# Adding the attention mask of 22 units by a TensorE product, with one maximum over four blocks and exponentials that read PSUM

## The chip, the cores and the metric

The kernel runs on one core of one Trainium2 chip. The metric is the device time of one execution in microseconds (us); lower is better. Each figure for a kernel is the median of some runs, and one more execution of it is profiled.

## What is computed

Three stages follow one another on 2304 tokens (4 sequences of 576) with 8 heads of 64:

```python
scores = scale * q @ k.T                      # scale = 1/8
scores = where(mask, scores, -1e9)            # heads 0-3: the last 32 keys
                                              # heads 4-7: every 4th of the last 128
attn = exp(scores - max(scores)); attn /= sum(attn) + 1e-9
x = attn @ v                                  # 2304 x 512
h = x @ w_in;  x = (h - tanh(h)) @ w_out      # 512 -> 2048 -> 512
h = x @ w_in2; s = h * softmax(h)             # 512 -> 1024
out = ((s - mean(s)) / sqrt(var(s) + 1e-6) * g_ln) @ w_out2
```

## The kernel before

**Units.** The attention is cut into 48 units. A unit holds four blocks; a block is 96 queries against the 128 keys that its mask can reach, so a unit's scores are a tile of 96 partitions x 512 columns (4 blocks x 128 keys), which is one PSUM bank. Eight units make the attention input of one group of 384 tokens, and there are six groups. `load_unit` (lines 123 to 130) brings a unit's transposed q and k (`qkr`, two buffers) and its v by two transfers on the SP queue; because `qkr` has two buffers, the transfer for unit u+2 waits until TensorE has read unit u.

**One unit, step by step** for the first 22 units (`qk_f32`, lines 151 to 166). TensorE multiplies the four blocks as float32 (line 158; the trace counts each as two matmul records, eight to a unit). VectorE then does, block by block, a `tensor_tensor_reduce` (line 163) that reads the scores from PSUM and the mask from SBUF, adds them, scales by -1/8, writes the result to the SBUF tile `p` and its minimum to `nm`; in the trace each is a CUSTOM_DVE_ANT_0 with a READ_ACCUMULATOR2. ScalarE takes the exponential of each block of `p` in place with `nm` as bias and the row sum as accumulator (`sm_exp`, line 198). `sm_norm` (lines 201 to 206) makes the reciprocal of the sum on VectorE and multiplies `p` on GpSimd (POOL, line 205). `tr_pe` transposes the four blocks on TensorE (line 212), ScalarE copies them to SBUF as `pt` (line 218), and `pv_pe` multiplies two units with v (line 233); ScalarE and VectorE write the result in a high and a low part as `x` (lines 241 and 242). The units from 22 on go through `qk_half` with float32r products and keep their own mask step (line 187).

**The constants.** The identity and three masks are one 256 KB transfer into the tile `cst_sb` (line 248), third on the SP queue after unit 0's two transfers.

**Order of the work.** The schedule is manual: each engine executes its instructions in the order in which the program writes them. The first loop (lines 253 to 273, called the first loop below) does units 0 to 7 and, beside them, splits weights: `w_step` (lines 81 to 111) unpacks one 128x512 piece of `w_in` or `w_out` by five or six instructions on VectorE and two on ScalarE. Its PSUM tiles have two banks for scores, two for transposes and two for the v products.

The second loop (line 395 on) is a list of slots. An even slot does `mm1` (line 297, twelve 128x384 products of the first layer for one of 16 column pieces), an odd slot does `mm2` (line 324, twelve products of the second layer, five pieces later). The hidden piece passes through four steps: `tanh` on ScalarE (line 305), `sub` on VectorE (line 308), `hi` on ScalarE (line 311), `lo` on VectorE (line 314). `plan` (line 336 on) puts the attention work of units 8 to 47 into slots: scores in slot p, exponentials in p+1, the transposes of the unit before one or two slots later, the v product one slot after that. All three take their PSUM bank from one pool of two, `a_ps`, in turn. Until about slot 40 each slot also carries `w_step`s. The last stage (lines 424 on) is the second layer pair, again TensorE products with VectorE and ScalarE steps between them.

Of the kernel before, what the change touches and what calls it, by code (L numbers as in the profile page):

```python
# [7 lines left out]
F32 = mybir.dt.float32  # L8
F32R = mybir.dt.float32r
I32 = mybir.dt.int32  # L10
AF = mybir.ActivationFunctionType
ALU = mybir.AluOpType
# [9 lines left out]
NQ, NK = 96, 128  # L22
NU = 8
QC, KC = 4 * NQ, 4 * NK
# [13 lines left out]
def tile_kernel(ctx: ExitStack, tc: tile.TileContext, qk, vw, cst, w_in, w_out, w_in2, w_out2, g_ln, out):  # L38
    nc = tc.nc
    ctx.enter_context(tc.manual_schedule())  # L40

    const = ctx.enter_context(tc.tile_pool(name="const", bufs=1, side="left"))
# [3 lines left out]
    g_p = ctx.enter_context(tc.tile_pool(name="g", bufs=2, side="right"))  # L46
# [3 lines left out]

    y_dr = dr_p.tile([128, KD, NTOK], F32, name="y_dr")

    cst_sb = const.tile([128, 128 + 3 * NK], F32, name="cst_sb")
    ident = cst_sb[:, 0:128]
    masks = cst_sb[:NQ, 128:].rearrange("p (t k) -> p t k", t=3)

    def mask_of(u, j):

        g, r = divmod(u, NU)
        hp, bp = divmod(r, 2)  # L60
        if hp < 2:
            return 0 if (4 * g + 2 * bp + j) % 6 == 0 else 1
        return (0, 2, 1)[g % 3]
# [59 lines left out]
    def load_unit(u):  # L123
        if u < NU * NG:
            r = at_p.tile([128, QC + KC], F32, tag="qkr", name=f"qkr{u}")
            n = 64 if u < NFU else 128
            nc.sync.dma_start(out=r[:n], in_=qk[u, :n])
            v = at_p.tile([NK, 2, 2, D], F32, tag="v", name=f"v{u}", bufs=6)
            nc.sync.dma_start(out=v.rearrange("p b h d -> p (b h d)"), in_=vw[u])
            un[u] = dict(r=r, v=v)  # L130
# [15 lines left out]
    def new_p(u):  # L146
        d = un[u]
        d["p"] = at_p.tile([NQ, 4, NK], F32, tag="p", name=f"p{u}", bufs=3)
        for t in ("nm", "sm", "rs"):
            d[t] = at_p.tile([NQ, 4], F32, tag=t, name=f"{t}{u}")  # L150

    def qk_f32(u, pool, tag):

        d = un[u]
        new_p(u)
        ps = pool.tile([128, 512], F32, tag=tag, name=f"qkp{u}")[:NQ, 0:KC].rearrange("p (b k) -> p b k", b=4)
        for b in range(4):
            nc.tensor.matmul(ps[:, b], d["r"][:64, b * NQ:(b + 1) * NQ],  # L158
                             d["r"][:64, QC + b * NK:QC + (b + 1) * NK], start=True, stop=True)

        def then():
            for b in range(4):
                nc.vector.tensor_tensor_reduce(  # L163
                    out=d["p"][:, b], in0=ps[:, b], in1=masks[:, mask_of(u, b % 2)], op0=ALU.add, op1=ALU.min,
                    scale=-0.125, scalar=3.0e38, accum_out=d["nm"][:, b:b + 1])
        return then

    def qk_half(u, hf, pool, tag):
# [26 lines left out]
    def sm_exp(u, bs=range(4)):  # L195
        d = un[u]
        for b in bs:
            nc.scalar.activation(out=d["p"][:, b], in_=d["p"][:, b], func=AF.Exp, scale=-1.0,  # L198
                                 bias=d["nm"][:, b:b + 1], accum_out=d["sm"][:, b:b + 1])

    def sm_norm(u):
# [43 lines left out]

    st_ps = tc.alloc_tile_pool(name="st_ps", bufs=2, space=PSUM, side="left")
    load_unit(0)
    nc.sync.dma_start(out=cst_sb, in_=cst)
    load_unit(1)
    w_load()  # L250
    load_unit(2)
# [3 lines left out]
    for r in range(NU + 3):  # L255
        t = qk_f32(r, st_ps, "qk") if r < NU else None
        b1 = pv_pe(r - 4, st_ps, "pv") if r % 2 == 0 and 0 <= r - 4 < NU else None
        b2 = tr_pe(r - 2, st_ps, "tr") if 0 <= r - 2 < NU else None
        if r in SW:
            w_step()  # L260
        if t:
            t()
        if back:
            back()
        back = b1
        if t:
            sm_exp(r)
        if 0 <= r - 1 < NU:
            sm_norm(r - 1)
        if b2:  # L270
            b2()
        if r + 3 < NU + 2:
            load_unit(r + 3)
# [67 lines left out]
    def plan():  # L341


        ready = 0
        for u in range(u0, u1 + 2):
            p = 4 * u - 41 if u >= 2 * NU else (2, 6, 8, 12, 14, 16, 18, 20)[u - u0]
            q = p + 2 if u >= 2 * NU or u < u0 + 4 else p + 1
            if u < u1:
                at(p + 2, lambda u=u: preps.extend(prep_unit(u + 1)))
                for i in (2, 3, 3):  # L350
                    at(p + i, lambda: preps.pop(0)() if preps else None)
                if u < NFU:
                    piece(p, lambda u=u: qk_f32(u, a_ps, "at"))
                    at(p + 1, lambda u=u: sm_exp(u))
                    at(p + 2, lambda u=u: sm_norm(u))
                else:
                    piece(p, lambda u=u: qk_half(u, 0, a_ps, "at"))
                    at(p + 2, lambda u=u: sm_exp(u, (0, 1)))
                    piece(p + 1, lambda u=u: qk_half(u, 1, a_ps, "at"))
                    at(p + 3, lambda u=u: sm_exp(u, (2, 3)))  # L360
                    at(p + 4, lambda u=u: sm_norm(u))
                at(p + 1, lambda u=u: load_unit(u + 2))
            if u0 <= u - 1 < u1:
                piece(q, lambda u=u: tr_pe(u - 1, a_ps, "at"))
            if u % 2 and u0 <= u - 3 < u1:
                piece(q + 1, lambda u=u: pv_pe(u - 3, a_ps, "at"))
# [194 lines left out]
def _layout(q, k, v, moe_w_in, moe_w_out, moe2_w_in, moe2_w_out, moe2_g_ln):  # L561
    import numpy as np

    def blocks(a, n, back):


        a = np.asarray(a)
        pl = a[:, :H // 2].transpose(1, 0, 2, 3).reshape(H // 2, B * S, D)
        di = a[:, H // 2:].reshape(B, H // 2, S // DIL, DIL, D).transpose(1, 3, 0, 2, 4)
        di = di.reshape(H // 2, DIL, B * S // DIL, D)  # L570
        o = np.zeros((NG, NU, 2, 2, n, D), a.dtype)
        for g in range(NG):
            for r in range(NU):
                hp, bp = divmod(r, 2)
                for h in range(2):
                    for b in range(2):
                        j = 2 * bp + b
                        if hp < 2:
                            t0, src = g * G + j * NQ - back, pl[2 * hp + h]
                        else:  # L580
                            t0, src = g * NQ - back, di[2 * (hp - 2) + h, j]
                        z = max(0, -t0)
                        o[g, r, h, b, z:] = src[t0 + z:t0 + n]
        return o.reshape(NG * NU, 2, 2, n, D)

    qb, kb, vb = blocks(q, NQ, 0), blocks(k, NK, WIN), blocks(v, NK, WIN)
    qkt = np.concatenate([qb.transpose(0, 4, 1, 2, 3).reshape(NG * NU, D, QC),
                          kb.transpose(0, 4, 1, 2, 3).reshape(NG * NU, D, KC)], axis=2)
    qkt = np.concatenate([qkt, qkt], axis=1)
    vt = vb.transpose(0, 3, 2, 1, 4).reshape(NG * NU, NK, 4 * D)  # L590

    def bits(w):
        return np.ascontiguousarray(w).view(np.int64)

    cst = np.zeros((128, 128 + 3 * NK), np.float32)
    cst[:, :128] = np.eye(128)
    qq, kk = np.arange(128)[:, None], np.arange(NK)[None]
    rel = qq + WIN - kk
    ok = (rel >= 0) & (rel < WIN)
    cross = (qq < NQ // 2) == (kk < WIN + NQ // 2)  # L600
    for i, m in enumerate((ok & (kk >= WIN), ok, ok & cross)):
        cst[:, 128 + i * NK:128 + (i + 1) * NK] = np.where(m, 0.0, -8.0e9)
    return dict(
        qk=qkt, vw=vt, cst=cst,
        w_in=bits(moe_w_in).reshape(KD, 128, NF, 128).transpose(2, 1, 0, 3).reshape(NF, 128, 512),
        w_out=bits(moe_w_out).reshape(NF, 128, DM),
        w_in2=bits(moe2_w_in).reshape(KD, 128, 2, 512).transpose(0, 2, 1, 3),
        w_out2=bits(moe2_w_out).reshape(NF2, 128, DM),
        g_ln=np.asarray(moe2_g_ln).reshape(NF2, 128).T,
    )  # L610
# [20 lines left out]
```

## Time and profile before

| | |
|---|---|
| median of three runs | 747.28 us (745.67 to 747.45) |
| profiled execution, its own time | 747.18 us |
| its span, first to last instruction | 745.4 us |
| TensorE busy | 717.0 us, 96% |
| VectorE busy | 490.8 us, 66% |
| ScalarE busy | 365.5 us, 49% |
| GpSimd busy | 134.7 us, 18% |
| mean granted TensorE clock | 0.995 |

Shares of busy time are averages over stages. The span has three: up to about 47 us the first loop with the loads, up to about 92 us a stretch of the second loop with dense `w_step`s, and the rest, which is TensorE work nearly without a gap. In a row of the timeline the first number is the start, the second the duration in us; durations of neighbours on one engine overlap a little, so the step from start to start is the cost of one. A note in square brackets gives the idle time before the row and what ended it.

### The profile page before, as it was taken

The page shows a single profiled execution, that of the slowest core. Times are in us where ns is not written, and L with a number is a line of the kernel's source. Part 1 is how long each engine was busy: PE and PEld are TensorE (multiplying, and loading weights), DVE is VectorE, ACT ScalarE, POOL GpSimd, SP SyncE. Part 2 cuts the span into 40 slices and gives each one's busy share as a digit, 9 for nine tenths or more (in the row PEclk, how much of TensorE's full clock was granted, in tenths as well). Part 3 has the DMA queues.
Part 4 walks back from the last instruction along what each step waited for, and adds up shares of the span by engine and source line. Part 5 has one row for each costly group of instructions (what it writes and reads, how often), then busy time and mean ns, then how long its engine had stood idle before and what let it go on. Part 6 is the DMA issues. An engine that isn't in the chain of part 4 may idle for free.

```text
span 745.4 us, 11617 instructions
## 1 busy us (share of the span) xinstructions
PE 717.0 (96%) x4168; PEld 653.4 (88%) x4168; DVE 490.8 (66%) x1273; ACT 365.5 (49%) x991; POOL 134.7 (18%) x187
## 2 busy tenths in 40 slices
PE   4968999999999999999999999999999999999997
PEld 3757899999999999999999999999888888888885
DVE  4889888746777777677777535797465555555452
ACT  4856676543444444354444423453255454535444
POOL 1622243201100111111111000020232312322110
PEclk9998999999999999999999999999999999999999
DMA  8857462122222212232212003733201101110001
GB/s 244 238 206 212 141 200 69 40 90 81 64 63 77 66 63 64 65 106 65 65 64 75 1 1 113 241 113 114 72 14 44 57 28 43 58 42 29 15 29 44
DMA packets 30186, 63.61 MB, mean 85 GB/s; under 512 B 2992, under 2 KB 16816, under 8 KB 30128
## 3 DMA queue, kind: packets, MB, share of 16 engines
q1 hardware_dynamic: 26960, 58.15, 24.8%
q10 hardware_dynamic: 3168, 4.72, 1.8%
q8 instruction: 33, 0.54, 0.3%
q14 instruction: 25, 0.20, 0.1%
HBM read 53.42 MB, written 9.44 MB: 84 GB/s over the span
## 4 chain that ended last, share of the span: by engine, by line
PE 88%; DVE 5%; ACT 3%; DMA 2%; POOL 1%; issue 1%; ACTq 0%; SPq 0%; POOLq 0%; DVEq 0%
PE y L324 26%; PE h L297 24%; PE po L524 14%; PE h L462 14%; PE qkp L158 3%; PE pv L233 2%; PE zt L505 2%; PE tp L212 2%; DMA qkr<-in_qk_dram 2%; PE qkp L178 2%; ACT p L198 1%; POOL p L205 1%; DVE gs L314 1%; DVE wi L85 1%; DVE p L163 1%
## 5 line engine op out<-in xcount | busy, mean ns | idle before, releaser
L297 PE MATMUL h<-x,wi 128*128 128x384 f32 x1152 | 223.5, 344 | 1.9 <-DVE x L242 1.8
L324 PE MATMUL y<-gs,wo 128*128 128x384 f32 x1152 | 217.3, 338 | 0.0
L297 PEld LDWEIGHTS h<-x,wi 128*128 128x128 f32 x1152 | 200.6, 191 | 4.0 <-DVE x L242 2.1
L324 PEld LDWEIGHTS y<-gs,wo 128*128 128x128 f32 x1152 | 198.0, 188 | 2.8
L205 POOL TENSOR_TENSOR p<-p,rs 96x512 f32<-96x512 f32 x48 | 77.8, 1621 | 351.3 <-DVE rs L204 259.0
L462 PE MATMUL h<-w2i,yt 128*128 128x512 f32 x432 | 104.9, 397 | 0.0
L524 PE MATMUL po<-w2o,z 128*128 128x512 f32 x432 | 104.1, 396 | 0.1
L524 PEld LDWEIGHTS po<-w2o,z 128*128 128x128 f32 x432 | 80.7, 188 | 20.4 <-ACT z L513 1.9
L513 ACT ACTIVATE z<-zt,gl_sb 128x128 fp32r<-128x128 f32 x144 | 51.0, 367 | 96.9 <-PE zt L505 48.6
L462 PEld LDWEIGHTS h<-w2i,yt 128*128 128x128 f32 x432 | 79.7, 187 | 18.4
L305 ACT ACTIVATE t<-h 128x384 f32<-128x384 f32 x96 | 47.1, 491 | 96.8 <-PE h L297 90.7
L514 DVE SCALAR_TENSOR_TENSOR z<-zt,gl_sb,z 128x128 fp32r<-128x128 f32 x144 | 48.9, 350 | 69.2 <-ACT z L513 69.2
L198 ACT ACTIVATE p<-p,nm 96x128 f32<-96x128 f32 x192 | 75.0, 392 | 32.8 <-DVE nm L163 32.8
L314 DVE TENSOR_TENSOR gs<-t,gs 128x384 fp32r<-128x384 f32 x96 | 75.7, 788 | 20.9 <-ACT gs L311 18.8
L308 DVE TENSOR_TENSOR t<-h,t 128x384 f32<-128x384 f32 x96 | 52.9, 551 | 32.4 <-ACT t L305 32.4
L311 ACT CAST gs<-t 128x384 fp32r<-128x384 f32 x96 | 49.2, 512 | 47.6 <-DVE t L308 47.5
L158 PE MATMUL qkp<-qkr 64*96 64x128 f32 x176 | 32.5, 340 | 15.6 <-DMA qkr<-in_qk_dram 11.2
L158 PEld LDWEIGHTS qkp<-qkr 64*96 64x96 f32 x176 | 26.7, 206 | 20.7 <-DMA qkr<-in_qk_dram 6.8
L242 DVE TENSOR_TENSOR x<-pv,x 128x384 fp32r<-128x384 f32 x24 | 16.9, 703 | 40.0 <-ACT x L241 40.0
L389 POOL TENSOR_TENSOR yt<-yr,yt 128x1024 fp32r<-128x1024 f32 x9 | 24.3, 2697 | 85.8 <-DVE yt L388 85.8
L479 DVE SCALAR_TENSOR_TENSOR u<-h,e 128x1024 f32<-128x1024 f32 x18 | 22.0, 1225 | 23.9 <-ACT e L478 23.9
L198 ACT ACTIVATION_READ_ACCUMULATOR p<-p,nm 96x1 f32 x192 | 36.2, 188 | 0.0
(68 smaller groups left out, 688.8 us busy)
## 6 DMA issues: line engine op xcount, KB each, us to landing
qkr<-in_qk_dram SPq DMA_DIRECT2D x26, 448.0 KB, 3.3
raw_wi<-in_w_in_dram SPq DMA_DIRECT2D x16, 512.0 KB, 6.4
raw_wo<-in_w_out_dram SPq DMA_DIRECT2D x16, 512.0 KB, 5.4
v<-in_vw_dram SPq DMA_DIRECT2D x48, 128.0 KB, 3.2
qkr<-in_qk_dram SPq DMA_DIRECT2D x22, 224.0 KB, 3.6
y_dr<-ys ACTq DMA_DIRECT2D x6, 768.0 KB, 3.8
yr<-y_dr SPq DMA_DIRECT2D x9, 512.0 KB, 4.4
out_dram<-o SPq DMA_DIRECT2D x18, 256.0 KB, 2.0
```

Source lines behind the costliest of these rows:

```text
L158: nc.tensor.matmul(ps[:, b], d["r"][:64, b * NQ:(b + 1) * NQ], d["r"][:64, QC + b * NK:QC + (b + 1) * NK], start=True, stop=True)
L198: nc.scalar.activation(out=d["p"][:, b], in_=d["p"][:, b], func=AF.Exp, scale=-1.0, bias=d["nm"][:, b:b + 1], accum_out=d["sm"][:, b:b + 1])
L205: nc.gpsimd.tensor_tensor(out=d["p"], in0=d["p"], in1=d["rs"].unsqueeze(2).to_broadcast([NQ, 4, NK]), op=ALU.mult)
L297: nc.tensor.matmul(ps, w[:, a, k * 128:(k + 1) * 128], xt[g, k][:, b], start=(n == 0), stop=(n == 3 * KD - 1))
L308: nc.vector.tensor_tensor(out=t, in0=ps, in1=t, op=ALU.subtract)
L311: nc.scalar.copy(out=gs[:, 0], in_=t)
L314: nc.vector.tensor_tensor(out=gs[:, 1], in0=t, in1=gs[:, 0].bitcast(F32), op=ALU.subtract)
L324: nc.tensor.matmul(yb[g][m], wo[c][:, a, m * 128:(m + 1) * 128], gs[:, b], start=(c == 0 and i == 0), stop=(c == NF - 1 and i == 2))
L462: nc.tensor.matmul(ps[:, n * 512:(n + 1) * 512], y[:, a, k, o:o + TT], w2i[2 * k + n][:, b], start=(q == 0), stop=(q == 3 * KD - 1))
L513: nc.scalar.activation(out=z[:, 0, c], in_=pp[n][:, j], func=AF.Copy, scale=gc)
L514: nc.vector.scalar_tensor_tensor(out=z[:, 1, c], in0=pp[n][:, j], scalar=gc, in1=z[:, 0, c].bitcast(F32), op0=ALU.mult, op1=ALU.subtract)
L524: nc.tensor.matmul(po, z[:, a, j], w2o[j][:, b], start=(q == 0), stop=(q == 3 * NF2 - 1))
```

## The change

Three things are changed, for units 0 to 21 alone. The mask is added by a TensorE product: a 96x96 identity times the masks, 512 columns in float32r, opens the PSUM accumulation, and the four float32 products accumulate onto it. VectorE takes one maximum over the last axis of the whole 96x512 tile (negated, into the four columns of `nm`) and multiplies `nm` by 1/8. The exponentials read the scores from PSUM with scale 1/8, and write `p`. For the product the constants must be of the float32r type, so they now land in a temporary tile `cst_f` and VectorE copies them to `cst_sb`. The mask value is -2^33 in place of -8e9.

```diff
-    cst_sb = const.tile([128, 128 + 3 * NK], F32, name="cst_sb")
-    ident = cst_sb[:, 0:128]
-    masks = cst_sb[:NQ, 128:].rearrange("p (t k) -> p t k", t=3)
+    cst_sb = const.tile([128, 128 + 3 * NK], F32R, name="cst_sb")
+    ident = cst_sb[:, 0:128].bitcast(F32)
+    rmasks = cst_sb[:NQ, 128:].rearrange("p (t k) -> p t k", t=3)
+    masks = cst_sb[:NQ, 128:].bitcast(F32).rearrange("p (t k) -> p t k", t=3)
...
         ps = pool.tile([128, 512], F32, tag=tag, name=f"qkp{u}")[:NQ, 0:KC].rearrange("p (b k) -> p b k", b=4)
+        m0, m1 = mask_of(u, 0), mask_of(u, 1)
+        if m0 != m1:
+            ms = rmasks[:, m0:m0 + 2].unsqueeze(1).to_broadcast([NQ, 2, 2, NK])
+        else:
+            ms = rmasks[:, m0:m0 + 1].to_broadcast([NQ, 4, NK])
+        nc.tensor.matmul(ps, cst_sb[:NQ, 0:NQ], ms, start=True, stop=False)
         for b in range(4):
             nc.tensor.matmul(ps[:, b], d["r"][:64, b * NQ:(b + 1) * NQ],
-                             d["r"][:64, QC + b * NK:QC + (b + 1) * NK], start=True, stop=True)
+                             d["r"][:64, QC + b * NK:QC + (b + 1) * NK], start=False, stop=(b == 3))
+        d["sc"] = ps
 
         def then():
-            for b in range(4):
-                nc.vector.tensor_tensor_reduce(
-                    out=d["p"][:, b], in0=ps[:, b], in1=masks[:, mask_of(u, b % 2)], op0=ALU.add, op1=ALU.min,
-                    scale=-0.125, scalar=3.0e38, accum_out=d["nm"][:, b:b + 1])
+            nc.vector.tensor_reduce(out=d["nm"], in_=ps, axis=mybir.AxisListType.X, op=ALU.max, negate=True)
+            nc.vector.tensor_scalar(out=d["nm"], in0=d["nm"], scalar1=0.125, scalar2=None, op0=ALU.mult)
         return then
...
         for b in bs:
-            nc.scalar.activation(out=d["p"][:, b], in_=d["p"][:, b], func=AF.Exp, scale=-1.0,
+            src, sc = (d["sc"], 0.125) if "sc" in d else (d["p"], -1.0)
+            nc.scalar.activation(out=d["p"][:, b], in_=src[:, b], func=AF.Exp, scale=sc,
                                  bias=d["nm"][:, b:b + 1], accum_out=d["sm"][:, b:b + 1])
...
-    nc.sync.dma_start(out=cst_sb, in_=cst)
+    cst_f = g_p.tile([128, 128 + 3 * NK], F32, tag="ys", name="cst_f", bufs=1)
+    nc.sync.dma_start(out=cst_f, in_=cst)
+    nc.vector.tensor_copy(out=cst_sb, in_=cst_f)
```

How the instructions stand on the engines shows at three places. A name such as `DVE_49` in square brackets is the semaphore of an engine or of a DMA queue on which the instruction waits.

First TensorE at the start of the program, units 0 and 1. Before:

```order
L158 MATMUL qkp_111<-qkr_86 96x128 [waits DMAHW0_49]
L158 MATMUL qkp_111<-qkr_86 96x128 x3
L158 MATMUL qkp_132<-qkr_91 96x128 [waits DMAHW3_49]
L158 MATMUL qkp_132<-qkr_91 96x128 x3
L158 MATMUL qkp_163<-qkr_97 96x128 [waits DMAHW6_49,DVE_49]
```

With the change:

```order
L164 MATMUL qkp_113<-cst_sb 96x512 [waits DVE_49]
L166 MATMUL qkp_113<-qkr_86 96x128 [waits DMAHW0_49]
L166 MATMUL qkp_113<-qkr_86 96x128 x3
L164 MATMUL qkp_133<-cst_sb 96x512
L166 MATMUL qkp_133<-qkr_93 96x128 [waits DMAHW3_49]
L164 MATMUL qkp_163<-cst_sb 96x512 [waits DVE_49,Activation_49]
```

Unit 0's products, which waited for unit 0's transfer alone, now stand behind a product that waits for VectorE's copy of the constants; and unit 2's bank is now waited for from ScalarE as well.

Second ScalarE at the start. Before:

```order
L198 ACT_TABLE_LOAD
L198 ACTIVATE p_107,sm_109<-p_107,nm_108 96x128 [waits DVE_49] x4
L92 ACTIVATE wa_wi_137<-raw_wi_95 128x512 [waits DMAHW5_49]
L198 ACTIVATE p_128,sm_130<-p_128,nm_129 96x128 [waits DVE_49] x4
L92 ACTIVATE wa_wi_174<-raw_wi_101 128x512 [waits DMAHW0_49]
```

With the change:

```order
L206 ACT_TABLE_LOAD [waits DVE_49]
L206 ACTIVATE p_109,sm_111<-qkp_113,nm_110 96x128 [waits PE_49]
L206 ACTIVATE p_109,sm_111<-qkp_113,nm_110 96x128 x3
L94 ACTIVATE wa_wi_139<-raw_wi_97 128x512 [waits DMAHW5_49]
L206 ACTIVATE p_129,sm_131<-qkp_133,nm_130 96x128 [waits DVE_49,PE_49]
```

The load of the function table waited for nothing and now carries the wait for the first maximum; the four exponentials of a unit, which waited each for its own block, now wait once for all four.

Third TensorE in the second loop, where the scores of unit 10 take the bank of unit 9 (`qkp_722` before, `qkp_714` with the change), and the transposes of unit 11 the bank of unit 12's scores (`tp_956` and `tp_947`). Before:

```order
L158 MATMUL qkp_722<-qkr_598 96x128 [waits DMAHW7_49,DVE_49]
L158 MATMUL qkp_722<-qkr_598 96x128 x3
...
L158 MATMUL qkp_913<-qkr_754 96x128 [waits DMAHW7_49,DVE_49]
L158 MATMUL qkp_913<-qkr_754 96x128 x3
...
L212 MATMUL tp_956<-cst_sb,p_840 128x96 [waits DVE_49,Pool_49]
```

With the change:

```order
L164 MATMUL qkp_714<-cst_sb 96x512 [waits DVE_49,Activation_49]
L166 MATMUL qkp_714<-qkr_591 96x128 [waits DMAHW7_49]
L166 MATMUL qkp_714<-qkr_591 96x128 x3
...
L164 MATMUL qkp_903<-cst_sb 96x512 [waits DVE_49,Activation_49]
...
L220 MATMUL tp_947<-cst_sb,p_831 128x96 [waits DVE_49,Activation_49,Pool_49]
```

Where TensorE waited for VectorE to have read a bank, it now also waits for ScalarE's exponentials out of it.

## Rows read from the trace of the kernel before

**Rows 1.** The page, its busy times and the span in 40 slices.
```profile
PE 717.0 (96%) x4168; PEld 653.4 (88%) x4168; DVE 490.8 (66%) x1273; ACT 365.5 (49%) x991; POOL 134.7 (18%) x187
...
PE   4968999999999999999999999999999999999997
```

**Rows 2.** Busy times by stretch: start:end, length, PE, PEld, DVE, ACT, POOL, clock, DMA, GB/s.
```profile
15.00:20.00 5.00, 1.97 (x9) 1.72 (x9) 2.81 (x14) 3.08 (x11) 2.27 (x1) 1.00 1.05 263
...
25.00:30.00 5.00, 4.60 (x22) 3.81 (x21) 4.27 (x18) 4.48 (x17) 3.34 (x2) 1.00 0.82 234
...
75.00:80.00 5.00, 5.00 (x31) 4.61 (x30) 4.92 (x11) 3.59 (x9) 1.04 (x1) 1.00 0.32 129
...
100.00:200.00 100.00, 100.00 (x659) 94.88 (x658) 69.71 (x205) 54.14 (x159) 20.99 (x11) 1.00 0.27 81
```

**Rows 3.** Timeline of TensorE, 0 to 62 us.
```profile
4.38 2.02 PE L158 MATMUL qkp<-qkr 64*96 64x128 f32 x8 [4.38 <-DMA qkr<-in_qk_dram]
...
18.04 1.99 PE L158 MATMUL qkp<-qkr 64*96 64x128 f32 x8 [3.21 <-DMA qkr<-in_qk_dram]
...
47.42 6.69 PE L297 MATMUL h<-x,wi 128*128 128x384 f32 x24 [1.83 <-DVE x L242]
54.05 1.11 PE L158 MATMUL qkp<-qkr 64*96 64x128 f32 x8
```

**Rows 4.** Timeline of the SP queue, unit 2's load.
```profile
6.43 0.47 SPq L127 DMA_DIRECT2D qkr<-in_qk_dram  x1
```

**Rows 5.** Timeline of VectorE: unit 0, then unit 9 in the second loop.
```profile
6.80 0.29 DVE L163 CUSTOM_DVE_ANT_0 p<-qkp,cst_sb 96x128 f32<-96x128 f32 x1 [6.80 <-DMA cst_sb<-in_cst_dram]
...
66.25 0.28 DVE L163 CUSTOM_DVE_ANT_0 p<-qkp,cst_sb 96x128 f32<-96x128 f32 x1
...
67.10 0.55 DVE L308 TENSOR_TENSOR t<-h,t 128x384 f32<-128x384 f32 x1
68.71 0.56 DVE L314 TENSOR_TENSOR gs<-t,gs 128x384 fp32r<-128x384 f32 x1 [1.07 <-ACT gs L311]
```

**Rows 6.** Timeline of ScalarE: start, unit 9, unit 13.
```profile
0.72 1.28 ACT L198 ACT_TABLE_LOAD   x1 [0.72 <-PEq L619]
...
66.63 0.40 ACT L198 ACTIVATE p<-p,nm 96x128 f32<-96x128 f32 x1 [1.86 <-DVE nm L163]
...
68.19 0.49 ACT L311 CAST gs<-t 128x384 fp32r<-128x384 f32 x1
...
94.26 0.39 ACT L198 ACTIVATE p<-p,nm 96x128 f32<-96x128 f32 x1
```

**Rows 7.** Timeline of TensorE, 60 to 130 us.
```profile
67.23 2.02 PE L158 MATMUL qkp<-qkr 64*96 64x128 f32 x8 [3.62 <-DVE nm L163]
...
88.28 0.52 PE L212 MATMUL tp<-cst_sb,p 96*128 96x96 f32 x4 [0.66 <-POOL p L205]
...
91.55 1.11 PE L158 MATMUL qkp<-qkr 64*96 64x128 f32 x8 [0.64 <-ACT pt L218]
...
97.32 0.88 PE L233 MATMUL pv<-pt,v 128*64 128x96 f32 x16
```

**Rows 8.** Groups by line and shape: names, shapes, count, busy us, mean ns.
```profile
L462 PE MATMUL h<-w2i,yt 128*128 128x512 f32 x432 | 104.9, 397 | 0.0
...
L477 DVE TENSOR_REDUCE sml<-h 128x1 f32<-128x1024 f32 x18 | 22.0, 1221 | 9.4 <-PE h L462 9.4
...
L163 DVE CUSTOM_DVE_ANT_0 p<-qkp,cst_sb 96x128 f32<-96x128 f32 x88 | 20.1, 282 | 12.6 <-DMA cst_sb<-in_cst_dram 6.8 <-PE qkp L158 5.8
...
L139 DVE CAST qks<-qkr 128x896 fp32r<-128x896 f32 x26 | 16.0, 614 | 0.0
...
L203 DVE TENSOR_SCALAR rs<-sm 96x4 f32<-96x4 f32 x48 | 8.4, 174 | 0.0
...
L163 DVE DVE_READ_ACCUMULATOR2_ANT nm<- 96x1 f32 x88 | 7.0, 79 | 0.0
...
L330 DVE COPY ys<-y 128x384 f32<-128x384 f32 x12 | 6.6, 556 | 8.5 <-PE y L324 8.5
```

More of the change, by code (lines that the diff above doesn't have):

```diff
@@ L601, in _layout @@
     for i, m in enumerate((ok & (kk >= WIN), ok, ok & cross)):
-        cst[:, 128 + i * NK:128 + (i + 1) * NK] = np.where(m, 0.0, -8.0e9)
+        cst[:, 128 + i * NK:128 + (i + 1) * NK] = np.where(m, 0.0, -2.0 ** 33)
     return dict(
```

## The prediction

> **What bounds the kernel now.** I read the page's shares first: TensorE is 96% busy over the span, and only its first five slices or so fall short [rows 1]. The table by stretch says when: from 100 to 200 us TensorE is busy for 100.00 of 100 us, so whatever is added to it there is paid in full. Before that other things bind: the DMA engines' share is 1.05 at 15 to 20 us, and VectorE is busy 4.92 of 5 us at 75 to 80 [rows 2]. So I price the change in three places.
>
> In the first 47 us the timeline of TensorE shows products that wait for transfers (unit 0's at 4.38 us, unit 3's at 18.04 us after 3.21 idle), and the hidden products begin at 47.42 us [rows 3]. From there to about 92 us VectorE is the bound: its instructions follow one another, and where it idles it is for ScalarE (1.07 us before line 314 at 68.71) [rows 5], while TensorE waits 3.62 us for unit 9's bank and 0.64 us for a copy that ScalarE makes late [rows 7]. After 91.55 us TensorE is the bound.
>
> **VectorE's step itself: nothing.** It falls from eight instructions to two. The old step takes from 66.25 to 67.10, 0.85 us from its start to the next instruction [rows 5]. The new maximum reads 512 columns of PSUM: the copy of 384 takes 556 ns and the reduction of 1024 takes 1221 [rows 8], so 1.04 ns per column and 556 + 128 x 1.04 = 0.69 us; the multiplication of 96x4 is like line 203, 0.17 [rows 8]. Together 0.86, less some 0.04 of overlap with the next: 0.82. That is 0.03 us less per unit.
>
> The Trainium skill, "VectorE: DVE Perf Modes", Rules for kernel authors, says to minimize the number of operations on VectorE. By that rule eight to two is a clear gain. The rows say that the old eight overlap; the rule's result is a rival below.
>
> **The start: 3.2 us.** The first maximum had to wait for the constants until 6.80 us [rows 5], while unit 0's products were long done. Now the products stand behind them too. The cast of 128x512 takes about 0.4 us (614 ns for 896 columns [rows 8]). The mask product is 128x512 in line 462, 104.9 / 432 = 0.243 us [rows 8]. Early TensorE work runs at half speed: the eight records of line 158 take 1.99 and 2.02 us here and 1.11 us at 54.05 [rows 3]. The granted clock in the table reads 1.00 (2.4 GHz) for all of these [rows 2]; I go by the durations, and price a mask product at 0.44 us before 47 us. So unit 0's products run from 6.80 + 0.4 + 0.44 + 0.1 = 7.7 and end at 9.7 us; they ended at 6.40 [rows 3]. Behind that end the SP queue holds unit 2's load, issued at 6.43 [rows 4], and behind it three 512 KB weight loads: all 3.3 us later. Bounds for what reaches unit 3's load are 0 (the DMA engines move what is queued and lose nothing) and 3.3. They are full at 15 to 20 us [rows 2], which is near the upper end, but the 512 KB queued last is 2.0 us of work at that row's 263 GB/s, so they do not stand for all of it: I take 2.1.
>
> From unit 3 on the path runs through TensorE (units 4 and 5), VectorE, POOL, then unit 7 on TensorE again; it meets three more mask products, 3 x 0.44 = 1.3, less 0.2 of waits that they fill: 1.1. Sum 3.2; bounds 1.1 and 4.6. The table load, 1.28 us at 0.72 us [rows 6], now starts after the first maximum. It delays unit 0's exponentials and with them unit 2's bank; I cost it at nothing, since unit 3 waits for its load meanwhile. Without that cover it is up to 1.3 more.
>
> **The VectorE stretch, units 8 to 12: 2.9 us.** The old exponentials begin 0.38 us after the first of the four steps (66.25 to 66.63 [rows 5, 6]), since block 0 needs its own minimum only. Now they need 0.69 + 0.03 + 0.17 + 0.04 = 0.93 us: 0.55 later. Behind the four exponentials ScalarE's queue holds line 311 (68.19 [rows 6]), and VectorE's line 314 waits for that (68.71 after 1.07 idle [rows 5]). I went through the same timelines for all five: units 9 and 11 show the idle of 1.1 us, and for the other three ScalarE's line 311 ends no earlier than VectorE is free. So each costs 0.55 - 0.03 = 0.52, 2.6 in all. Bounds are 0 and 0.55 each.
>
> The held banks come on top. Unit 10's products took unit 9's bank when VectorE had read it, at 67.23 [rows 7]; now they wait for the exponentials, 1.6 us longer. TensorE runs behind nothing there, and the five mask products of this stretch (0.24 each, 0.44 while slow) hide in the same waits, so both cost nothing; if that cover were gone, they are 1.4 for the products. One place reaches the path: the transposes at 88.28 [rows 7] take unit 12's bank, now free some 1.6 us later, and twelve products stand between them and 91.55; of the idle 0.66 and 0.64 there nothing is left and I count 0.3 more. Sum 2.9; bounds 0 and 4.5.
>
> **TensorE from 92 us on: 2.2 us.** Units 13 to 21 are nine mask products at 0.243, on a TensorE without gaps. Bounds 0.21 each (a share by columns of the same row's busy time, were some of it start-up) and 0.30.
>
> **Sum:** 3.2 + 2.9 + 2.2 = 8.3 us. On the profiled execution's own 747.18 us that is 755.5; it is 0.1 us below the median of the runs, so no correction.
>
> **Rivals.**
> 1. *The start is absorbed* by the transfer queue; only the mask products on the path stay, 1.1 in place of 3.2: 753.4 us. For it: 2.0 us of data are still queued when the load is late. Against: TensorE's 3.21 us wait for unit 3's load [rows 3].
> 2. *Held banks stall TensorE after 92 us as well.* Unit 13's last exponential begins at 94.26 [rows 6] and ends at 94.65; the v product that takes its bank next starts at 97.32 [rows 7]. That is 2.7 us of room, of which 0.55 goes. About four places are of this kind. If each lost 1 us, it would be 759.5. It decides once ScalarE lags by over 2 us. The Trainium skill, "PSUM: Partial Sum Buffer", Summary: rules for kernel authors, says to evacuate promptly, which speaks against this change; by rows 6 and 7 the delay fits in that room.
> 3. *TensorE comes up to full speed early.* The mask product is a full-width pass of 512 columns between short ones. If durations from unit 3 on were those of 54.05 us, units 3, 4, 5 and 7 on the path give back 0.9 each (1.99 against 1.11), the first 24 hidden products 2.0 (6.69 us [rows 3] against 4.72 for 24 at full speed, twice line 297's step of 2.36), three mask products 0.6: 6.2, so 749.3. Against: at 25 to 30 us TensorE is busy for 4.60 of 5 us [rows 2] and still slow.
> 4. *Not slower: VectorE's instruction count is what costs.* If the eight old instructions occupied 4 x (0.282 + 0.079) [rows 8] = 1.44 us and the new two 0.86, each unit would save 0.58. Over five units the VectorE stretch would give 2.9 back in place of costing 2.9, and the two maxima on the path of the first loop 1.2: 8.3 - 5.8 - 1.2 = 1.3, so 748.5, no change that can be told. It decides if the timeline's 0.85 understates the step. Against: start-to-start times are what the next instruction sees. That is the result by the skill's rule on the number of operations, named above.
>
> **How the numbers follow.** A measurement of this kernel can tell about 0.3% (2.2 us) from no change. The forecast has 0.60, with a range of its own from 752.5 to 758; rival 1 has 0.14, rival 2 0.10, rival 3 0.07, rival 4 0.06, and 0.03 is left for faster by more, two of them together. Slower is 0.60 + 0.14 + 0.10 = 0.84; rivals 3 and 4 make 0.13 for the same; faster 0.03. The range from 751.5 to 759 holds the forecast, rival 1 and half of rival 2, about 0.79.
>
> **What would show it.** Each step has its mark: the first product on TensorE near 7.3 us and unit 0's end near 9.7; ACT_TABLE_LOAD near 10.7; unit 3's four products near 20; the first hidden product near 50.6; a TENSOR_REDUCE of 0.69 us; exponentials that begin 0.9 us after it starts; unit 13's products near 97.6; 22 mask products, the last nine 0.24 us apart from their neighbours. I am wrong if the hidden products start before 49 us, if VectorE's line 314 does not slip behind the exponentials, or if TensorE shows idle time over 1 us after 100 us.

## The result and the profile after

The change takes 755.1 us (median of four runs, 753.51 to 757.42) beside 746.89 for the kernel before: a ratio of 1.0111 with a 95% interval from 1.0094 to 1.0127, so 8.2 us slower, between 7.0 and 9.5. The forecast was 755.5, slower.

The profiled execution of the change is the slowest of its four runs, 757.42 us with a span of 755.6. Its time lies 2.3 us above their median. That matters below: where those 2.3 us lie has to be found before its rows are read.

First the page of the change: busy times, then the same TensorE slices as in [rows 1].

```profile
PE 724.5 (96%) x4190; PEld 657.0 (87%) x4190; DVE 489.4 (65%) x1142; ACT 361.4 (48%) x991; POOL 134.7 (18%) x187
...
PE   4767999999999999999999999999999999999997
```

TensorE has its 22 products more (4168 to 4190) and is 7.5 us longer busy. VectorE runs 131 instructions fewer, and is busy for 1.4 us less: eight records became two, and almost no time went with them. The new instructions in the groups by line (shapes, count, busy us, mean ns, idle before):

```profile
L206 ACT ACTIVATE p<-qkp,nm 96x128 f32<-96x128 f32 x88 | 30.9, 357 | 41.4 <-DVE nm L172 32.9 <-DVE rs L211 7.5 <-PE tp L220 0.9
...
L171 DVE TENSOR_REDUCE nm<-qkp 96x4 f32<-96x512 f32 x22 | 15.0, 682 | 13.6 <-PE qkp L166 13.5
L164 PE MATMUL qkp<-cst_sb 96*96 96x512 f32 x22 | 11.9, 541 | 12.9 <-DVE cst_sb L258 6.5 <-ACT p L206 6.4
```

The timeline of TensorE in the change, from its first product to unit 14's (the mask product is line 164, the four score products line 166, the hidden layer line 307):

```profile
6.53 0.74 PE L164 MATMUL qkp<-cst_sb 96*96 96x512 f32 x1 [6.53 <-DVE cst_sb L258]
7.20 2.02 PE L166 MATMUL qkp<-qkr 64*96 64x128 f32 x8
...
13.06 0.74 PE L164 MATMUL qkp<-cst_sb 96*96 96x512 f32 x1 [1.23 <-ACT p L206]
...
21.55 2.02 PE L166 MATMUL qkp<-qkr 64*96 64x128 f32 x8 [4.54 <-DMA qkr<-in_qk_dram]
...
25.98 2.02 PE L166 MATMUL qkp<-qkr 64*96 64x128 f32 x8 [1.15 <-DMA qkr<-in_qk_dram]
...
52.90 6.38 PE L307 MATMUL h<-x,wi 128*128 128x384 f32 x24 [1.84 <-DVE x L250]
...
74.71 0.74 PE L164 MATMUL qkp<-cst_sb 96*96 96x512 f32 x1 [5.18 <-ACT p L206]
...
99.77 0.40 PE L164 MATMUL qkp<-cst_sb 96*96 96x512 f32 x1
```

Against [rows 3]: unit 0's products start at 7.20 instead of 4.38, unit 3's (21.55) still wait for their load, and unit 4's (25.98) now wait for theirs too. Before, unit 4's waited for no load:

```profile
21.02 1.99 PE L158 MATMUL qkp<-qkr 64*96 64x128 f32 x8 [0.17 <-DVE nm L163]
```

The hidden products begin at 52.90, not 47.42. On the SP queue (start, duration) unit 2's load, behind the first score products, goes out at 9.24 instead of 6.43 [rows 4], unit 4's at 15.78:

```profile
9.24 0.47 SPq L129 DMA_DIRECT2D qkr<-in_qk_dram  x1
...
15.78 0.47 SPq L129 DMA_DIRECT2D qkr<-in_qk_dram  x1
```

The table by stretch of the change (columns as in [rows 2]) shows what that does. The DMA engines stand idle from 8 to 10 us, at a share of 0.01; from 15 to 20 us they are full again, but over the first 20 us they moved 202 GB/s in the mean, beside 246 before, so the gap isn't made up by then. The last row is the stretch without gaps on TensorE, as before:

```profile
8.00:10.00 2.00, 2.00 (x8) 1.29 (x8) 0.71 (x2) 0.00 (x0) 0.00 (x0) 1.00 0.01 4
15.00:20.00 5.00, 2.01 (x9) 1.23 (x7) 4.15 (x10) 2.38 (x10) 1.39 (x1) 1.00 1.05 278
...
100.00:200.00 100.00, 100.00 (x658) 93.66 (x657) 68.63 (x155) 53.20 (x161) 23.66 (x11) 1.00 0.30 89
```

VectorE around unit 9's maximum in the change, the place of [rows 5]:

```profile
72.17 0.68 DVE L171 TENSOR_REDUCE nm<-qkp 96x4 f32<-96x512 f32 x1
72.88 0.17 DVE L172 TENSOR_SCALAR nm<-nm 96x4 f32<-96x4 f32 x1
72.96 0.55 DVE L318 TENSOR_TENSOR t<-h,t 128x384 f32<-128x384 f32 x1
75.09 0.56 DVE L324 TENSOR_TENSOR gs<-t,gs 128x384 fp32r<-128x384 f32 x1 [1.58 <-ACT gs L321]
...
82.12 0.56 DVE L324 TENSOR_TENSOR gs<-t,gs 128x384 fp32r<-128x384 f32 x1 [0.54 <-ACT gs L321]
...
91.71 0.56 DVE L324 TENSOR_TENSOR gs<-t,gs 128x384 fp32r<-128x384 f32 x1 [1.59 <-ACT gs L321]
```

Before, line 314 of unit 11, which stands in the place of the last of these rows:

```profile
84.33 0.56 DVE L314 TENSOR_TENSOR gs<-t,gs 128x384 fp32r<-128x384 f32 x1 [1.10 <-ACT gs L311]
```

And ScalarE in the change, at the start and at that same maximum [rows 6]:

```profile
10.22 1.28 ACT L206 ACT_TABLE_LOAD   x1 [10.22 <-DVE nm L172]
...
73.17 0.36 ACT L206 ACTIVATE p<-qkp,nm 96x128 f32<-96x128 f32 x1 [2.47 <-DVE nm L172]
...
74.55 0.51 ACT L321 CAST gs<-t 128x384 fp32r<-128x384 f32 x1
```

The new step holds VectorE from 72.17 to 72.96, 0.79 us, where the old one took 0.85. Its exponentials begin 1.00 us after its start (old: 0.38), the cast of line 321 waits behind them, and VectorE's line 324 (314 before) stands idle for 1.58 us instead of 1.07.

Two marks on TensorE divide the span into three: the first hidden product, and unit 13's first product (scores before, mask now). For before they are 47.42 and 91.55 of a span of 745.4; for the change 52.90 and 99.77 of 755.6.

| us | start | to unit 13 | rest | sum |
|---|---|---|---|---|
| before | 47.42 | 44.13 | 653.85 | 745.4 |
| the change | 52.90 | 46.87 | 655.83 | 755.6 |
| difference | 5.5 | 2.7 | 2.0 | 10.2 |
| predicted | 3.2 | 2.9 | 2.2 | 8.3 |

Two terms came out as forecast. The start is 2.3 us too long, just what this execution is above its median, but one profile can't say whether that is the change or chance. The experiments are on that, and on which part of the change pays for each stretch.

### The profile page after: what moved, and what is told of

Read it like the earlier page. It is cut to its first block, busy times and chain, and to the rows that moved or that the text cites. A ratio compares the mean times of both kernels' runs of the same rounds, so it can differ in the third digit from the quotient of the medians.

```text
span 755.6 us, 11526 instructions
## 1 busy us (share of the span) xinstructions
PE 724.5 (96%) x4190; PEld 657.0 (87%) x4190; DVE 489.4 (65%) x1142; ACT 361.4 (48%) x991; POOL 134.7 (18%) x187
## 4 chain that ended last, share of the span: by engine, by line
PE 90%; DVE 3%; ACT 2%; DMA 2%; POOL 1%; issue 1%; ACTq 0%; SPq 0%; POOLq 0%
PE y L334 26%; PE h L307 25%; PE po L534 13%; PE h L472 13%; PE qkp L166 3%; PE pv L241 2%; PE zt L515 2%; PE tp L220 2%; PE qkp L185 2%; DMA qkr<-in_qk_dram 1%; PE qkp L164 1%; ACT p L206 1%; POOL p L213 1%; DMA cst_f<-in_cst_dram 1%; DVE nm L171 0%
## 5 line engine op out<-in xcount | busy, mean ns | idle before, releaser
L206 ACT ACTIVATE p<-qkp,nm 96x128 f32<-96x128 f32 x88 | 30.9, 357 | 41.4 <-DVE nm L172 32.9
L206 ACT ACTIVATE p<-p,nm 96x128 f32<-96x128 f32 x104 | 40.7, 393 | 0.0
```

The source lines that it names most:

```text
L206: nc.scalar.activation(out=d["p"][:, b], in_=src[:, b], func=AF.Exp, scale=sc, bias=d["nm"][:, b:b + 1], accum_out=d["sm"][:, b:b + 1])
```

## The experiments

Changes of the median are against the kernel before in the same session: 747.39 us (23 runs) for the first four experiments, 746.8 (21) for the next four, 747.63 (7) for the last three.

**Parts of the change by unit.** A set NEW holds the units that go the new way; the others keep the four old products and the four fused additions with their minima.

```diff
+        if u not in NEW:
+            for b in range(4):
+                nc.tensor.matmul(ps[:, b], d["r"][:64, b * NQ:(b + 1) * NQ],
+                                 d["r"][:64, QC + b * NK:QC + (b + 1) * NK], start=True, stop=True)
...
+            return old
```

*NEW = range(0, 8): the start alone.*

> The new path for units 0 to 7 only; units 8 to 21 as before. Theory (the terms add up, and the start is the term that was sized too small): this kernel alone carries the start. In the profile of the change the hidden products begin at 52.90 us instead of 47.42, so about +5.5 us against the kernel before, first hidden product near 52.9. Rival (the sum on record): +3.2 us, first hidden product near 50.6. Rival (the start costs nothing by itself, the whole loss is in the second loop): within 1 us of before.

749.75 us, ratio 1.0031 [1.0018, 1.0043], +2.4. The first hidden product starts at 49.40, not at 52.90, and unit 3's products wait 1.92 us for their load:

```profile
19.27 2.02 PE L178 MATMUL qkp<-qkr 64*96 64x128 f32 x8 [1.92 <-DMA qkr<-in_qk_dram]
```

That is the start as forecast or a little less, and not the 5.5 of the profile of the change.

*NEW = range(8, 22): all but the start.*

> The new path for units 8 to 21 only; units 0 to 7 as before, the cast of the constants stays. Theory: the start is as before (first hidden product within 0.7 us of 47.42), the VectorE stretch costs 2.7 to 2.9 and the nine products behind it 2.0 to 2.2, so +4.7 to +5.1 us. Rival (held banks or late exponentials cost nothing, only products count): +2.2. Rival (all of the loss is the start): within 1 us of before.

752.2 us, 1.0064 [1.0048, 1.0079], +4.8, as expected; the stretch to unit 13 is 46.69. The first hidden product stands at 48.25, 0.83 us behind that of the kernel before where I had expected it within 0.7. With the start alone it makes 7.2, inside the interval of the whole change.

*NEW = range(13, 22): the units where TensorE is the bound.*

> The new path for units 13 to 21 only, which all lie behind 92 us, where TensorE has no gaps. Theory: nine mask products of 0.22 to 0.243 us, +2.0 to +2.2 us. Rival (late exponentials and held banks stall TensorE there too): over +4 us and waits of mask products for exponentials in the trace. Rival (the mask products find gaps): within 0.7 us of before.

749.46 us, 1.0029 [1.0018, 1.0039], +2.1: nine mask products at 0.23.

*The same nine units without their mask product,* so that their scores stay unmasked.

```diff
-        nc.tensor.matmul(ps, cst_sb[:NQ, 0:NQ], ms, start=True, stop=False)
...
-                start=False, stop=(b == 3))
+                start=True, stop=True)
```

> As the new path for units 13 to 21 only, but without the mask product there, so that these units' scores are unmasked; one maximum and exponentials out of PSUM stay. Theory: the products were the whole cost behind 92 us, so within 0.7 us of before. Rival (held banks): what is left of the cost of the run with the products stays, +1 us or more.

746.98 us, 0.9996 [0.9984, 1.0008]: nothing left. So after 92 us the product is the whole cost. The late exponentials and the banks that they hold cost nothing there that these runs can tell, and the fewer instructions on VectorE bring nothing there.

**The start.** *NEW = range(1, 22): unit 0 the old way.*

> The change, but unit 0 goes the old way: its products do not wait for the constants, its exponentials do not read PSUM, and the function table is loaded at the start. Theory: the start's 5.5 us fall to the mask products on the path, 3 x 0.44 less filled waits, about 1.1; first hidden product near 48.5 to 49; total +5.5 to +6.5 us against before (the change: +8.2). Rival (the start's cost lies in the mask products and the late exponentials of units 1 to 7): no better than the change by more than 1 us.

752.65 us, 1.0071 [1.0055, 1.0088], +5.85: 2.35 less than the change, as expected. In its SP queue unit 2's load is back where it was, and on its TensorE the hidden products begin at 48.79:

```profile
6.03 0.47 SPq L130 DMA_DIRECT2D qkr<-in_qk_dram  x1
```
```profile
48.79 7.17 PE L319 MATMUL h<-x,wi 128*128 128x384 f32 x24 [1.84 <-DVE x L262]
```

Unit 0 going the new way is thus most of the start's cost. The edit gives back its old products, its load order, its additions and its exponentials together, so that it is the load behind the products that costs is read from the rows, not parted from the rest by a run.

*The table loaded early,* by an exponential of 96x1 ahead of everything:

```diff
+    tb = at_p.tile([NQ, 1], F32, tag="tb", name="tb", bufs=1)
+    nc.vector.memset(tb, 0.0)
+    nc.scalar.activation(out=tb, in_=tb, func=AF.Exp)
     load_unit(0)
```

> The change, with one exponential of a 96x1 tile of zeros ahead of the program's first transfer, so that the function table is loaded at the start instead of behind the first maximum. Theory (in the profile of the change the chain runs through the table load, unit 0's exponentials, unit 2's bank and unit 4's transfer): unit 2's products end 1.2 to 1.3 us earlier, unit 4's arrive earlier by 1 us or more, and the time falls by 1.0 to 1.5 us against the change, to about +7 over before. By the prediction on record (the load is covered by unit 3's wait): no change against the change, +8.2.

754.82 us, 1.0102 [1.0088, 1.0116], +8.0: no gain that can be told, although the interval (6.6 to 8.7) still holds the +7 of my theory. The marks decide against it: the first hidden product starts at 50.67, within the range of the change's own starts (52.90, and 50.12 in its second profile below). The table is loaded at 0.72 us, as before the change, and ScalarE's first exponential starts right behind the maximum; but TensorE's unit 3 still waits for its transfer:

```profile
0.72 1.28 ACT L257 ACT_TABLE_LOAD   x1 [0.72 <-PEq L632]
...
10.52 0.36 ACT L206 ACTIVATE p<-qkp,nm 96x128 f32<-96x128 f32 x1 [8.30 <-DVE nm L172]
```
```profile
20.42 2.02 PE L166 MATMUL qkp<-qkr 64*96 64x128 f32 x8 [4.14 <-DMA qkr<-in_qk_dram]
```

TensorE reaches this wait 1.56 us earlier than in the second profile of the change (unit 3's mask product at 15.55 and 17.11), and waits 4.14 us there instead of 2.16: what the early table gave went into the wait for the data. The cover that the prediction named held.

*Weights out of the way, in the kernel before:* two of the three 512 KB weight loads ahead of the loop move behind the unit loads of its passes 3 and 5.

```diff
-    for _ in range(3):
-        w_load()
+    w_load()
...
         if r + 3 < NU + 2:
             load_unit(r + 3)
+        if r in (3, 5):
+            w_load()
```

> The kernel before, with two of the three weight loads that stand together behind unit 2's transfer moved behind units 6 and 8, so that 1 MB less is queued ahead of unit 3's transfer. Theory (in the first 20 us the transfers bind and a late or crowded transfer of q and k reaches the path in full): unit 3's products start 2 to 4 us earlier than 18.04, the first hidden product 1 to 3 us earlier, 1 to 3 us less in all. Rival (what is moved is only paid later, since VectorE or the loads bind from 20 us on): no change, or slower by up to 3 us because weight pieces come late.

745.41 us (11 runs), 0.9983 [0.9974, 0.9992]: 1.4 us faster than the kernel before, and the fastest kernel here. On its TensorE, unit 3's products come 3.48 us earlier than in [rows 3], and half of that reaches the hidden products:

```profile
14.56 1.99 PE L158 MATMUL qkp<-qkr 64*96 64x128 f32 x8 [0.24 <-DMA qkr<-in_qk_dram]
...
45.74 6.21 PE L298 MATMUL h<-x,wi 128*128 128x384 f32 x24 [1.84 <-DVE x L242]
```

So before the change, unit 3's load does stand on the path, and the weights in the queue are part of it.

*The change again,* and *the same spread in the change* (the diff above on it), in one session:

> The change itself once more, with another profile. Theory (52.90 us for the first hidden product is a draw of the transfers: kernels that share its start gave 50.27 and 49.40, kernels that share the old start 47.42 to 48.34): the first hidden product comes between 49.4 and 51.5, behind unit 4's transfer, and the stretch from there to unit 13 takes 46.9 us as in the first profile, within 0.3. Rival (52.90 is what the change does): again above 52.

> The change, with the same two weight loads moved back as in the run on the kernel before. Theory (what the start costs is a late transfer that is then crowded): unit 3's products start within 17 us instead of 19.3 to 21.6 in the profiles of the change's start so far, the first hidden product near 48.5 to 49.5 instead of 49.4 to 52.9, and the time is 1.5 to 3 us less than the change, +5 to +6.5 over before. Rival (mask products and late exponentials set the start): no change against the change.

The change again: 754.76 us, 1.01 [1.008, 1.0121]. Its stretch to unit 13 is 46.86 and its rest 655.82, both within 0.01 us of the first profile; its start is not. On TensorE:

```profile
20.00 2.02 PE L166 MATMUL qkp<-qkr 64*96 64x128 f32 x8 [2.16 <-DMA qkr<-in_qk_dram]
...
23.20 2.02 PE L166 MATMUL qkp<-qkr 64*96 64x128 f32 x8
...
50.12 6.49 PE L307 MATMUL h<-x,wi 128*128 128x384 f32 x24 [1.83 <-DVE x L250]
```

Unit 4's products no longer wait. The 52.90 of the first profile was one slow draw of the transfers: there unit 4's load took 10.15 us in the chain of waits.

With the spread, 753.61 us, 1.0087 [1.007, 1.0104]: 6.0 above the kernel before, as expected, but only 1.15 below the change of that session, where I had 1.5 to 3, with run times that overlap. The marks were missed too: I had unit 3's products within 17 us and the hidden ones at 48.5 to 49.5, and they start at 18.58 and 50.51. This profile is of the slowest of the four runs, 1.4 us above their median. Its chain of waits (start, us, what) shows what held it up:

```profile
13.92 7.10 DMA raw_wi<-in_w_in_dram
21.05 0.59 DVE wy_wi L95
21.64 0.60 DVE wy_wi L103
22.23 0.60 DVE wy_wi L107
22.84 0.61 DVE nm L171
```

The weight tile, loaded later, now holds up VectorE's weight work, and unit 3's maximum stands behind that. In this execution what the units' loads gave was lost to the weights: the wait moved. Whether the faster three runs lost as much is not shown.

**The stretch of VectorE, units 8 to 12.** *Without the maximum* (no maximum, no multiplication, exponentials with bias 0 in units 8 to 12):

```diff
-            nc.vector.tensor_reduce(out=d["nm"], in_=ps, axis=mybir.AxisListType.X, op=ALU.max, negate=True)
+            if u not in NOMAX:
+                nc.vector.tensor_reduce(out=d["nm"], in_=ps, axis=mybir.AxisListType.X, op=ALU.max, negate=True)
...
-                bias=d["nm"][:, b:b + 1]
+                bias=0.0 if u in NOMAX else d["nm"][:, b:b + 1]
```

> The change, but units 8 to 12 leave out the maximum: VectorE does nothing for them, and their exponentials start when the products end, with bias 0. Theory (in the stretch to 92 us VectorE is the bound, and each unit's exponentials delay ScalarE's line for the high part, on which VectorE waits): five times VectorE's 0.82 us plus up to five times the 0.55 us of lateness come off, so 4 to 7 us less than the change, +1 to +4 over before; VectorE's idle before the low part falls below 0.6 us per unit. Rival (TensorE's waits for held banks bound the stretch): under 2 us less than the change.

748.22 us, 1.0015 [1.0004, 1.0026], +1.4: 6.8 us less than the change, as expected. The stretch shrinks to 40.41 us, by 6.5. Five steps of 0.79 are 4.0 of that. The rest is less idle time of VectorE before the low part: 4.8 us over the five units in the change, 1.2 here, where units 9 and 11 alone still wait, 0.58 each. Together that is 1.1 us more than the stretch lost, so not all of it reached TensorE's mark.

```profile
69.24 0.56 DVE L326 TENSOR_TENSOR gs<-t,gs 128x384 fp32r<-128x384 f32 x1 [0.58 <-ACT gs L323]
```

*With the maximum, but exponentials that don't use it* (only the bias is 0):

```diff
-                bias=d["nm"][:, b:b + 1]
+                bias=0.0 if u in FREE else d["nm"][:, b:b + 1]
```

> The change, but the exponentials of units 8 to 12 use bias 0 and so do not wait for the maximum, which VectorE still takes for them. It parts lateness from VectorE's time, both of which the run without the maximum took away together (6.9 us less than the change). Theory (lateness is on the path in each of the five units): the exponentials no longer hold up ScalarE's line for the high part, so VectorE's idle before the low part goes from 0.54 and 1.59 us to near 0: 2.7 to 5 us less than the change. Rival (VectorE's own time alone counts): under 1 us less than the change.

752.84 us, 1.0072 [1.0057, 1.0087]: 1.9 less than the change of its session, between the two expectations. The edit did less than I meant. ScalarE's first exponential of unit 9 still starts behind the maximum, not behind its own products; both read the same bank. First ScalarE, then VectorE of that kernel:

```profile
70.64 0.27 ACT L207 ACTIVATE p<-qkp 96x128 f32<-96x128 f32 x1 [2.24 <-DVE nm L172]
```
```profile
69.87 0.68 DVE L172 TENSOR_REDUCE nm<-qkp 96x4 f32<-96x512 f32 x1
70.58 0.17 DVE L173 TENSOR_SCALAR nm<-nm 96x4 f32<-96x4 f32 x1
70.66 0.55 DVE L319 TENSOR_TENSOR t<-h,t 128x384 f32<-128x384 f32 x1
72.20 0.56 DVE L325 TENSOR_TENSOR gs<-t,gs 128x384 fp32r<-128x384 f32 x1 [0.99 <-ACT gs L322]
```

So only the wait for the multiplication went (the exponential begins 0.77 us after the maximum's start, not 1.00) and each exponential is 0.27 long instead of 0.36. ScalarE is done 0.23 + 4 x 0.09 = 0.6 us earlier, while VectorE's own work is unchanged. The idle time before line 325 falls from 1.58 to 0.99, the same 0.6, and the stretch from 46.86 to 44.26: nearly that of the kernel before, 44.13. VectorE did the same, ScalarE ended earlier, and 2.6 of the 2.7 us were gone. The time shows 1.9 of them; the start of this profile is a late one, with the first hidden product at 51.20.

## Why the prediction was right, step by step

**The bound and the direction: right.** Each of the three stretches cost about what its own bound says, and an experiment on each took most or all of its cost away.

**VectorE's step, 0.82 for 0.85: right.** It is 0.79. The maximum takes 0.68 (0.69 forecast), so the price per column that came from a copy and a longer reduction holds. Rival 4, that the number of instructions costs, is out: the step is 0.06 us shorter, not 0.58, VectorE's busy time fell by 1.4 us in all for 131 instructions, and the stretch that VectorE bounds became longer. The Trainium skill, "VectorE: DVE Perf Modes", Rules for kernel authors, says to minimize the number of operations, in its row on chained operations. Taken as a rule for any eight instructions, as rival 4 took it, it promised a gain that these runs don't show: the eight belong to four independent blocks and overlap each other.

**The start, 3.2: right, with errors that offset each other.** Alone it costs 2.4 us (interval 1.3 to 3.2); the whole less the other units is 8.2 - 4.8 = 3.4. Two steps of it can be checked. The load behind unit 0 was put at 2.1, and unit 0 alone gives back 2.35; in the second profile of the change unit 3's products come 1.96 us later than before. The table load was put at nothing, and loading it early gave nothing that can be told. One price was wrong: a mask product at half speed lasts 0.67 us from its start to that of the score products (6.53 to 7.20), not 0.44. At unit 0 this did not show, because the constants came somewhat earlier than I had it: the first product starts at 6.53 to 7.35 in the six profiles with the new start, mean 7.0, against 7.3. Behind unit 3 it was luck. Three mask products at that price are 2.0 us, and 0.2 was to come off for waits that they fill; but from unit 3's products to the first hidden one the second profile has 30.12 us, the kernel before 29.38. That is 0.74, less than the 1.1 forecast, so about 1.3 us of the products fell into waits. The mark "50.6" fits: these six have the first hidden product at 49.40 to 52.90, mean 50.8; four with the old one at 47.42 to 48.34, mean 48.1. Between the means lie 2.7 us. Three of those four old starts are of kernels that already copy the constants, and their profiled runs are 0.7 to 1.1 us above their own medians. With each profile's distance from its kernel's median taken off its mark (an estimate: it puts all of that distance at the start), the means are 50.5 and 47.4, 3.0 apart. The single profile of before that I worked from had the earliest start of its four, that of the change the latest of its six.

**The VectorE stretch, 2.9: right.** 2.7 us. From unit 9's line 314 to unit 11's, two units on, it was 84.33 - 68.71 = 15.62 us; now it is 91.71 - 75.09 = 16.62, so 0.50 per unit, against 0.52. Five units make 2.5; the 0.2 left agrees with the 0.3 put on the bank of unit 12, but no run parts it. One detail was different: all five units now wait, units 8, 10 and 12 for 0.54 us. The exponentials start later than I had it (1.00 instead of 0.93) but run shorter, 357 ns on PSUM against 393 for those that still read SBUF.

**TensorE from 92 us, 2.2: right.** The rest of the span is 653.56 to 653.85 us in the four profiles without mask products there (mean 653.71) and 655.72 to 656.24 in the nine with them (mean 655.90): 2.19 us, or 0.243 for each of nine, which is the price taken from line 462. From start to start a mask product reads 0.33 or 0.40 there (99.77 to 100.10, 106.68 to 107.08), so the length of the stretch, not the single record, gives the price.

**The other rivals.** Absorbed transfers (rival 1): unit 0 alone is worth 2.35 us, so no. Held banks (rival 2): TensorE waits for one at 74.71 for 5.18 us, but from 100 to 200 us it is busy for 100.00, and without the products nothing is left; out. The Trainium skill, "PSUM: Partial Sum Buffer", Summary: rules for kernel authors, wants banks evacuated promptly; here, from 92 us on, the later release cost nothing that these runs can tell. TensorE early at full speed (rival 3): unit 4's products still take 2.02 us and the first 24 hidden ones 6.38; out.

## What to carry to other kernels

Price a change by the stretch and its bound: the same edit cost 0.24 us per unit where TensorE was full, 0.5 where VectorE waited for ScalarE, and at the start 2.35 us for the one unit that had to wait for the constants, with a load queued behind it. Fewer instructions are no gain where the old ones overlap, and one reduction over four blocks makes the first block's consumer wait for the last. Before a profile's crowded start is read to the microsecond, take a second profile of the same kernel.

## What was not expected of the hardware

The start of one and the same code differs by as much as the effects in it: the first hidden product of the change came at 52.90 in one profile and at 50.12 in another, with the rest of the program equal to 0.01 us. What sets the speed of a transfer there stays open; unit 4's took 10.15 us in the slow one.

The load of the exponential's table stands behind the wait of the first exponential: at 0.72 us before, when nothing was awaited by it, at 10.22 in the change. And two engines that only read one PSUM bank still ran one after the other: with no data from the maximum in it, the exponential began 0.09 us after the maximum ended. The row puts the end of its wait down to the maximum (<-DVE nm L172), which points to a wait of the program; whether the chip would demand it was not tried.

The granted clock is not enough to tell TensorE's speed. In the profile of the change it reads 1.00 (2.4 GHz) from 0 to 50 us and 0.50 (1.2 GHz) from 75 to 80 us, and a unit's score products take 2.02 us in both (at 7.20 above, and at 75.38), against 1.11 at 59.45:

```profile
0.00:50.00 50.00, 32.07 (x158) 24.23 (x160) 29.22 (x69) 26.46 (x93) 20.59 (x12) 1.00 0.82 229
75.00:80.00 5.00, 5.00 (x17) 4.34 (x17) 4.84 (x12) 2.82 (x10) 2.85 (x1) 0.50 0.25 62
```
```profile
59.45 1.11 PE L166 MATMUL qkp<-qkr 64*96 64x128 f32 x8
...
75.38 2.02 PE L166 MATMUL qkp<-qkr 64*96 64x128 f32 x8
```
